# Weights prepared later and two at a time: the order of the weight split in a fused attention and MoE kernel

## The chip, the cores and the metric

One core of a Trainium2 chip runs the kernel. The metric is the device time of one execution in microseconds; the figure for a kernel is the median of its runs. Engine names below are those of the profile: PE is the matmul engine (PEld its weight loads), DVE the vector engine, ACT the scalar engine, POOL the GpSimd engine, SP the engine that issues most DMAs.

## What is computed

The reference runs a windowed attention with sink columns over 4 batches, 8 heads, 768 positions and a head size of 64, and sends the result through one gated two-layer block ("MoE" below, with a single expert):

```
scores = scale * q @ k^T, masked to (key < n_sink) or (0 <= query - key < window)
a = softmax(scores);  x = (a @ v), heads side by side: 3072 tokens x 512
out = ((x @ w_a) * (x @ w_b)) @ w_out          w_a, w_b: 512 x 1536, w_out: 1536 x 512
```

The three weights arrive in 64-bit floating point, so that each weight value is two 32-bit words, `lo` and `hi`. The rest is fp32.

## The kernel before, in words

The tokens are cut into eight chunks of 2 to 4 tiles of 128 rows (`CHUNKS`). `run` (L732 on) first computes the attention of chunk 0 alone (`first`, 4 tiles, 8 heads: 32 units of a head and a tile). Then `moe` (L674 on) works on one chunk after the other, and in the middle of the MoE of chunk c the generator `between` takes steps of the attention of chunk c+1. The matmuls of the MoE split each fp32 operand into a high and a low part of type fp32r and take three products (high by high, high by low, low by high).

The weights are cut into 12 blocks of each kind: `a` (w_a), `b` (w_b) and `o` (w_out), 128 x 512 values each, 36 in all. The MoE loop over j uses a_j (`half`, L685), then b_j, then o of j-1 (`project`, L694). For every block the kernel does the following, in four stages, each pinned in program order:

- `load_weight` (L289): one DMA of 512 KB into a raw tile;
- `weight_bits` (L297 to L299): two DVE operations on the high words and, between them, an ACT operation that scales the low words in place (L298);
- `weight_sum` (L307): a DVE integer addition that joins both;
- `weight_high` (L313): an ACT cast to fp32r, which writes the high part;
- `weight_low` (L318): a DVE subtraction, which writes the low part.

The high and low parts take the place of the raw tile in memory. `weights_to` moves this conveyor by steps: step k does bits of block k, sum of block k-1, high of block k-2 and low of block k-3. In the first attention a step is taken at every third generator step from `STEP0` = 18 on (18, 21, ..., 36: seven steps); in the first MoE one step is taken before every a, b and o. The order of the blocks is a0 b0 o0 a1 b1 o1 and so on.

In the attention of chunk 0 a unit's score matmul (L547) goes into PSUM; DVE takes the mask and the row minimum (L554); ACT takes the exponent (L556); DVE forms the sum's reciprocal (L558, L559) and multiplies (L561); PE transposes (L584); ACT copies (L585, tile ptx); PE multiplies with v (L601). The sink columns go through sct (L614), sk (L623) and an addition (L625). The head pairs' results xf are split into xh (ACT, L666) and xl (DVE, L667), which the first MoE matmuls read. PE, DVE and ACT each take their instructions strictly in order; a scheduler decides that order when the kernel is built, within the pins.

Of the kernel before, what the change touches and what calls it, by code (L numbers as in the profile page):

```python
# [7 lines left out]
F32 = mybir.dt.float32  # L8
BF16 = mybir.dt.bfloat16
F32R = mybir.dt.float32r  # L10
I32 = mybir.dt.int32
# [206 lines left out]
class Fast:  # L218
# [14 lines left out]
    def consts(self):  # L233
# [18 lines left out]
        self.wt, self.raw, self.wf, self.unchecked = {}, {}, {}, []  # L252

    def masks(self, val):

# [28 lines left out]
    def src(self, kind):  # L284
        return {"a": self.wa, "b": self.wb, "o": self.wo}[kind]

    def load_weight(self, kind, j):
        raw = self.wp.tile([P, 2 * DM], I32, tag=f"w_{kind}{j}", name=f"raw_{kind}{j}")
        self.nc.sync.dma_start(raw, self.src(kind)[j].bitcast(I32))  # L289
        self.raw[kind, j] = raw  # L290

    def weight_bits(self, kind, j):
        nc, pin = self.nc, self.tc.keep_in_program_order
        rv = self.raw[kind, j].rearrange("p (n c) -> p n c", c=2)
        lo, hi = rv[:, :, 0], rv[:, :, 1]
        f = self.io([P, DM], I32, f"wf_{kind}{j}")
# [4 lines left out]
        self.wf[kind, j] = f  # L301

    def weight_sum(self, kind, j):

        f = self.wf[kind, j]
        lo = self.raw.pop((kind, j)).rearrange("p (n c) -> p n c", c=2)[:, :, 0]
        self.tc.keep_in_program_order(self.nc.vector.tensor_tensor(f, f, lo, op=ALU.add))  # L307
        self.wf[kind, j] = f.bitcast(F32)

    def weight_high(self, kind, j):  # L310
        w = self.wp.tile([P, 2, DM], F32R, tag=f"w_{kind}{j}", name=f"w_{kind}{j}")
        self.wt[kind, j] = (w[:, 0, :], w[:, 1, :])
        self.tc.keep_in_program_order(self.nc.scalar.copy(w[:, 0, :], self.wf[kind, j]))  # L313

    def weight_low(self, kind, j):
        wh, wl = self.wt[kind, j]
        self.tc.keep_in_program_order(
            self.nc.vector.tensor_tensor(wl, self.wf.pop((kind, j)), wh.bitcast(F32), op=ALU.subtract))  # L318

    def check_weight(self, kind, j):  # L320

# [349 lines left out]
    def moe(self, row, nt, xf, between, weights_ahead, last, weights_split):  # L671
# [4 lines left out]
        outs = [self.ps.tile([P, DM], F32, tag=("o0", "o1", "o2", "av")[i], name=f"o{tag}_{i}") for i in range(nt)]  # L676

        def half(kind, j):
            wh, wl = self.wt[kind, j]
            ps = self.ps.tile([P, 4 * P], F32, tag=kind, name=f"{kind}{tag}_{j}")  # L680
            for kk in range(NK):
                ksl = slice(kk * P, (kk + 1) * P)
                xh, xl = xs[kk]
                for i, (w, x) in enumerate(((wh, xh), (wh, xl), (wl, xh))):
                    nc.tensor.matmul(ps[:, :n], lhsT=w[:, ksl], rhs=x[:, :n],  # L685
                                     start=kk == 0 and i == 0, stop=kk == NK - 1 and i == 2)
            return ps

        def project(j, gh, gl):
            wh, wl = self.wt["o", j]  # L690
# [40 lines left out]

    def run(self, scalars, verdict):  # L732
        chunks = CHUNKS
        order = [(k, j) for j in range(NJ) for k in "abo"]
        done, loaded = [0], [0]

        def weights_to(n, ahead):
            while loaded[0] < min(n + ahead, len(order)):
                self.load_weight(*order[loaded[0]])
                loaded[0] += 1  # L740
            while done[0] < min(n + D2, len(order) + D2):
                k = done[0]
# [7 lines left out]
        pairs = [self.wp.tile([P, 2, nt * P], F32, tag=f"w_{k}{NJ - 1}", name=f"xf0_{k}") for k in "bo"]  # L750
        xf = [x[:, i, :] for x in pairs for i in range(2)]
        first = self.attention(b, t0, nt, xf, exact=True, alone=True)
        next(first)
        val = scalars()
# [112 lines left out]
```

## Time and profile before

| | us |
|---|---|
| median of 3 runs | 802.18 |
| lowest and highest run | 800.78, 804.23 |
| the profiled execution, its own time | 800.92 |
| span of its trace, first to last instruction | 799.0 |

PE is busy for 785.5 us of the span, DVE for 433.3, ACT for 475.8 and POOL for 307.1. The chain of work that ended last lies on PE for 92% of the span, on DVE for 4% and on ACT for 3%. A matmul's busy time in such a trace has its pipeline in it: matmuls that follow each other start closer together than each one lasts, so that a gap of a few tenths of a microsecond between them does not show as idle time. What PE really takes for a group is read from the starts of the groups.

### The profile page before, as it was taken

How to read it: one execution, taken by the hardware profiler on the slowest of the kernel's cores; microseconds unless marked ns; L12 is line 12 of the kernel's file. 1: busy time of each engine (PE TensorE's matmuls, PEld its weight loads, DVE VectorE, ACT ScalarE, POOL GpSimd, SP SyncE). 2: the span in 40 equal slices, each digit the busy share in tenths (PEclk: the TensorE clock that was granted, in tenths of full speed). 3: DMA queues.
4: the chain of work that ended last, by engine and by line, in shares of the span. 5: the costliest groups of instructions: out<-in, count | busy, mean ns of one | idle time of the engine just before them, and what ended most of it. 6: DMA issues, size and time to landing. Idle time of an engine off the chain costs nothing.

```text
span 799.0 us, 13573 instructions
## 1 busy us (share of the span) xinstructions
PE 785.5 (98%) x4457; PEld 697.2 (87%) x4457; DVE 433.3 (54%) x1485; ACT 475.8 (60%) x1384; POOL 307.1 (38%) x425
## 2 busy tenths in 40 slices
PE   8989999999999999999999999999999999999997
PEld 5657777779899999999999999999999999999996
DVE  6889988835654565445653555535654457430101
ACT  5877676527764676467764777646764677641111
POOL 1111100416672644546642565606635366201120
PEclk9999999999999999999999999999999999999999
DMA  8868610122221242313333143322333132000001
GB/s 314 298 228 319 205 30 1 41 82 77 61 73 38 79 128 90 104 55 117 102 102 116 42 123 109 91 77 64 114 119 102 54 107 61 1 14 28 1 1 42
DMA packets 44779, 76.12 MB, mean 95 GB/s; under 512 B 4640, under 2 KB 24224, under 8 KB 44704
## 3 DMA queue, kind: packets, MB, share of 16 engines
q1 hardware_dynamic: 41648, 69.70, 27.2%
q10 hardware_dynamic: 3024, 5.51, 1.8%
q8 instruction: 36, 0.59, 0.3%
q14 instruction: 39, 0.32, 0.1%
q0 software_dynamic: 32, 0.00, 0.0%
HBM read 68.90 MB, written 6.29 MB: 94 GB/s over the span
## 4 chain that ended last, share of the span: by engine, by line
PE 92%; DVE 4%; ACT 3%; DMA 1%; issue 1%; POOL 0%; DVEq 0%; POOLq 0%; ACTq 0%
PE a L685 25%; PE o L694 24%; PE b L685 24%; PE t L450 4%; PE s L418 4%; PE av L466 3%; PE s L547 2%; PE av L601 2%; PE t L584 1%; PE t L601 1%; PE sk L491 1%; ACT p L425 1%; DVE g L710 0%; ACT xf L471 0%; DVE xf L472 0%
## 5 line engine op out<-in xcount | busy, mean ns | idle before, releaser
L685 PE MATMUL a<-xh,w_a 128*128 128x384 f32 (+2 forms) x768 | 218.2, 345 | 1.3 <-ACT xh L666 1.0
L685 PE MATMUL b<-xh,w_b 128*128 128x384 f32 (+2 forms) x768 | 215.8, 343 | 0.0
L694 PE MATMUL o<-w_o,gh 128*128 128x512 f32 x576 | 186.9, 404 | 0.0
L685 PEld LDWEIGHTS a<-xh,w_a 128*128 128x128 f32 x768 | 138.8, 188 | 8.2 <-issue 1.7
L715 POOL TENSOR_TENSOR gl<-g,gh 128x384 fp32r<-128x384 f32 (+1 forms) x70 | 68.2, 974 | 201.1 <-ACT gh L713 198.3
L685 PEld LDWEIGHTS b<-xh,w_b 128*128 128x128 f32 x768 | 138.8, 188 | 4.7 <-issue 1.2
L710 DVE TENSOR_TENSOR g<-b,g 128x384 f32<-128x384 f32 (+2 forms) x96 | 53.4, 557 | 146.2 <-PE b L685 133.3
L685 PE MATMUL b<-xl,w_b 128*128 128x384 f32 (+2 forms) x384 | 129.2, 336 | 0.0
L685 PE MATMUL a<-xl,w_a 128*128 128x384 f32 (+2 forms) x384 | 129.2, 336 | 0.0
L694 PEld LDWEIGHTS o<-w_o,gh 128*128 128x128 f32 x576 | 104.0, 188 | 19.3 <-issue 0.8
L694 PE MATMUL o<-w_o,gl 128*128 128x512 f32 x288 | 113.6, 395 | 0.0
L713 ACT CAST gh<-g 128x384 fp32r<-128x384 f32 (+2 forms) x96 | 49.3, 514 | 78.4 <-DVE g L710 76.5
L704 ACT COPY g<-a 128x384 f32<-128x384 f32 (+2 forms) x96 | 45.2, 471 | 72.9 <-PE a L685 70.3
L429 ACT ACTIVATE p<-p,st 128x128 f32<-128x128 f32 (+1 forms) x144 | 71.4, 496 | 26.4 <-DVE st L428 25.5
L425 ACT ACTIVATE p<-p,st 128x128 f32<-128x128 f32 (+1 forms) x144 | 71.6, 497 | 8.5 <-DVE st L423 8.4
L685 PEld LDWEIGHTS a<-xl,w_a 128*128 128x128 f32 x384 | 72.4, 189 | 2.3
L685 PEld LDWEIGHTS b<-xl,w_b 128*128 128x128 f32 x384 | 72.4, 188 | 1.6
L453 ACT CAST pt<-t 128x128 fp32r<-128x128 f32 (+1 forms) x144 | 50.4, 350 | 39.1 <-PE t L450 37.3
L454 DVE TENSOR_TENSOR pt<-t,pt 128x128 fp32r<-128x128 f32 (+1 forms) x144 | 57.2, 397 | 20.7 <-ACT pt L453 19.2
L694 PEld LDWEIGHTS o<-w_o,gl 128*128 128x128 f32 x288 | 54.1, 188 | 13.1 <-DVE gl L715 0.8
L568 POOL COPY sc<-p 128x8 f32<-128x8 f32 x32 | 15.7, 490 | 128.7 <-ACT p L563 86.6
L423 DVE CUSTOM_DVE_ANT_0 p<-s,mg 128x264 f32<-128x264 f32 x96 | 41.1, 429 | 34.2 <-PE s L418 34.0
(141 smaller groups left out, 1287.3 us busy)
## 6 DMA issues: line engine op xcount, KB each, us to landing
qr<-in_qT_dram SPq DMA_DIRECT2D x48, 192.0 KB, 2.6
raw_a<-in_wa_dram SPq DMA_DIRECT2D x12, 512.0 KB, 6.5
raw_b<-in_wb_dram SPq DMA_DIRECT2D x12, 512.0 KB, 6.6
raw_o<-in_wo_dram SPq DMA_DIRECT2D x12, 512.0 KB, 6.6
chk_a<-in_wa_dram SPq DMA_DIRECT2D x24, 256.0 KB, 2.7
chk_b<-in_wb_dram SPq DMA_DIRECT2D x24, 256.0 KB, 2.7
chk_o<-in_wo_dram SPq DMA_DIRECT2D x24, 256.0 KB, 2.8
out_dram<-os ACTq DMA_DIRECT2D x21, 256.0 KB, 2.1
```

The source lines that it names most:

```text
L418: nc.tensor.matmul(ps[:, :w], lhsT=q[:, i * P:(i + 1) * P], rhs=ks[:, c0:c0 + w], start=m == 0, stop=m == 1)
L423: nc.vector.tensor_tensor_reduce(out=p[:, :w], in0=ps[:, :w], in1=m, scale=-0.125, scalar=BIG, op0=ALU.add, op1=ALU.min, accum_out=st[:, 0:1])
L425: nc.scalar.activation(p[:, :w], p[:, :w], AF.Exp, bias=st[:, 0:1], scale=-1.0, accum_out=st[:, 1:2])
L429: nc.scalar.mul(p[:, :w], p[:, :w], st[:, 3:4])
L453: nc.scalar.copy(hs, tp[:, :n, :])
L454: nc.vector.tensor_tensor(ls, tp[:, :n, :], hs.bitcast(F32), op=ALU.subtract)
L685: nc.tensor.matmul(ps[:, :n], lhsT=w[:, ksl], rhs=x[:, :n], start=kk == 0 and i == 0, stop=kk == NK - 1 and i == 2)
L694: nc.tensor.matmul(outs[i], lhsT=g[:, sl], rhs=w, start=j == 0 and k == 0, stop=j == NJ - 1 and k == 2)
L704: nc.scalar.copy(g[:, :n], pa[:, :n])
L710: nc.vector.tensor_tensor(g[:, :n], pb[:, :n], g[:, :n], op=ALU.mult)
L713: nc.scalar.copy(gh[:, :n], g[:, :n])
L715: e.tensor_tensor(gl[:, :n], g[:, :n], gh[:, :n].bitcast(F32), op=ALU.subtract)
```

## The change

The order of the blocks becomes the order of their first use: a0 b0 a1 b1 o0 a2 b2 o1 and so on. In the first attention the steps begin at generator step 24 (24, 27, ..., 36: five steps). Blocks 0 and 1 and the last eight (28 to 35) go through the stages singly, as before. Blocks 2 to 27 go in 13 pairs: one raw tile holds two blocks, and each of the two bits operations, the ACT scaling, the sum, the cast and the subtraction works on 1024 words a partition instead of 512. For a pair, sum and high are issued in the same step, one after the bits, and low one step later. The pairs' intermediate value is one tile of its own in the weight pool (named wf), so the last four blocks, two of which use its place, are loaded only when the last pair is done. Before the product of a block in the MoE, low of the block three or four places later has been issued instead of four later.

```diff
-STEP0, STEPS = 18, 3
-AHEAD, LOADS = 3, 9
-D0, D1, D2 = 1, 2, 3
+STEP0, STEPS = 24, 3
+AHEAD, LOADS = 1, 11
+DELAY = 3
+SINGLE, PAIRS = 2, 14
...
+    def weight_bits(self, k, n):
         nc, pin = self.nc, self.tc.keep_in_program_order
...
+        lo, hi = self.words(k, n)
+        if n == 2:
+            if self.temp is None:
+
+                self.temp = self.wp.tile([P, 2 * DM], I32, tag=f"w{3 * NJ // 2 - 2}", name="wf")
+            f = self.temp
+        else:
+            f = self.io([P, DM], I32, f"wf{k}")
...
-        order = [(k, j) for j in range(NJ) for k in "abo"]
+
+        order = self.order = sorted(((k, j) for j in range(NJ) for k in "abo"), key=lambda w: 3 * w[1] + (0, 1, 5)["abo".index(w[0])])
...
+            wide = range(SINGLE, 2 * PAIRS)
             while loaded[0] < min(n + ahead, len(order)):
-                self.load_weight(*order[loaded[0]])
+                if loaded[0] >= len(order) - 4 and done[0] <= 2 * PAIRS:
+                    break
+                self.load_weight(loaded[0])
                 loaded[0] += 1
-            while done[0] < min(n + D2, len(order) + D2):
+            while done[0] < min(n + DELAY, len(order) + DELAY):
                 k = done[0]
-                for d, stage in ((D2, self.weight_low), (D1, self.weight_high), (D0, self.weight_sum), (0, self.weight_bits)):
-                    if 0 <= k - d < len(order):
-                        stage(*order[k - d])
                 done[0] += 1
+                singles = lambda d: 0 <= k - d < len(order) and k - d not in wide
+                if singles(3):
+                    self.weight_low(k - 3, 1)
+                if k % 2 == 0 and k - 2 in wide:
+                    self.weight_low(k - 2, 2)
+                if singles(2):
+                    self.weight_high(k - 2, 1)
+                if singles(1):
+                    self.weight_sum(k - 1, 1)
+                if k % 2 == 1 and k - 1 in wide:
+                    self.weight_sum(k - 1, 2)
+                    self.weight_high(k - 1, 2)
+                if singles(0):
+                    self.weight_bits(k, 1)
+                if k % 2 == 0 and k in wide:
+                    self.weight_bits(k, 2)
...
-                weights_to(done[0] + 1 - D2, 4 + D2)
+                weights_to(done[0] + 1 - DELAY, 4 + DELAY)
...
-                weights_to(max(s + AHEAD, done[0] + 1 - D2), LOADS)
+                weights_to(max(s + AHEAD, done[0] + 1 - DELAY), LOADS)
```

Line numbers from here on in the changed kernel are 17 higher in the attention and the MoE (L561 becomes L578, L666 becomes L683), and the weight stages move to L293 (load), L316 to L318 (bits), L325 (sum), L330 (high) and L335 (low).

The first place is the end of the first attention on DVE. A name such as p_0_7_2 is the softmax tile of chunk 0, head 7, tile 2; the last number of a name only counts tiles. Before, from the product of the last head's second tile to the first instruction behind that of its last tile:

```order
L561 TENSOR_SCALAR p_0_7_1_677<-p_0_7_1_677,st_0_7_1_678 128x264
L318 TENSOR_TENSOR w_b_624<-wf_b_518,w_b_624 128x512
L307 ISA wf_a_627<-raw_a_444,wf_a_627 128x1024
L297 TENSOR_SCALAR wf_b_694<-raw_b_446 128x512
L561 TENSOR_SCALAR p_0_7_2_700<-p_0_7_2_700,st_0_7_2_701 128x264
L299 SCALAR_TENSOR_TENSOR wf_b_694<-raw_b_446,wf_b_694 128x512
L558 TENSOR_SCALAR st_0_7_3_715<-st_0_7_3_715 128x1
L558 TENSOR_SCALAR st_4_0_0_879<-st_4_0_0_879 128x1
L559 RECIPROCAL st_0_7_3_715<-st_0_7_3_715 128x1
L559 RECIPROCAL st_4_0_0_879<-st_4_0_0_879 128x1
L561 TENSOR_SCALAR p_0_7_3_714<-p_0_7_3_714,st_0_7_3_715 128x264
L318 TENSOR_TENSOR w_o_691<-wf_o_576,w_o_691 128x512
```

With the change, the same stretch:

```order
L578 TENSOR_SCALAR p_0_7_1_654<-p_0_7_1_654,st_0_7_1_655 128x264
L325 ISA wf_604<-raw_549,wf_604 128x1024
L316 TENSOR_SCALAR wf<-raw_552 128x1024
L575 TENSOR_SCALAR st_0_7_2_677<-st_0_7_2_677 128x1
L575 TENSOR_SCALAR st_0_7_3_691<-st_0_7_3_691 128x1
L318 SCALAR_TENSOR_TENSOR wf<-raw_552,wf 128x1024
L576 RECIPROCAL st_0_7_2_677<-st_0_7_2_677 128x1
L576 RECIPROCAL st_0_7_3_691<-st_0_7_3_691 128x1
L684 TENSOR_TENSOR xl_2_765<-xf_117,xh_2_764 128x512
L578 TENSOR_SCALAR p_0_7_2_676<-p_0_7_2_676,st_0_7_2_677 128x264
L578 TENSOR_SCALAR p_0_7_3_690<-p_0_7_3_690,st_0_7_3_691 128x264
L335 TENSOR_TENSOR w_667<-wf_557,w_667 128x512
```

Ahead of the last product stood five bits, four sums and two subtractions of single blocks; now there are the bits of two single blocks and of one pair and two single sums. Low of the first block (w_667) has moved behind it.

The second place is the seam between attention and MoE on ACT, from the copy of the last head's result xf to the copy g_0 of the first a product. Before:

```order
L603 COPY xf_o<-av_0_7_756 64x512
L313 CAST w_b_773<-wf_b_694 128x512
L298 ACTIVATE raw_a_571<-raw_a_571 128x512
L585 COPY ptx_4_0_0_979<-t_4_0_0_980 128x256
L666 CAST xh_3_799<-xf_o 128x512
L313 CAST w_o_814<-wf_o_744 128x512
L298 ACTIVATE raw_b_621<-raw_b_621 128x512
L556 ACTIVATE p_4_0_1_924,st_4_0_1_925<-p_4_0_1_924,st_4_0_1_925 128x264
L704 COPY g_0_834<-a_0_821 128x512
```

With the change:

```order
L620 COPY xf_117<-av_0_7_728 64x512
L317 ACTIVATE raw_555<-raw_555 128x1024
L330 CAST w_718<-wf 128x1024
L573 ACTIVATE p_4_0_0_839,st_4_0_0_840<-p_4_0_0_839,st_4_0_0_840 128x264
L683 CAST xh_3_768<-xf_117 128x512
L721 COPY g_0_799<-a_0_786 128x512
```

The copy ptx_4_0_0 of the next chunk's first transposes no longer stands ahead of xh_3; an exponent and two operations on a pair do.

The third place is a piece of the first MoE on DVE, from the product g_2. Before:

```order
L710 TENSOR_TENSOR g_2_1029<-b_2_1054,g_2_1029 128x512
L299 SCALAR_TENSOR_TENSOR wf_a_990<-raw_a_809,wf_a_990 128x512
L318 TENSOR_TENSOR w_b_987<-wf_b_903,w_b_987 128x512
L307 ISA wf_a_990<-raw_a_809,wf_a_990 128x1024
L297 TENSOR_SCALAR wf_b_1012<-raw_b_811 128x512
L559 RECIPROCAL st_4_1_1_1034<-st_4_1_1_1034 128x1
L318 TENSOR_TENSOR w_o_1009<-wf_o_939,w_o_1009 128x512
L299 SCALAR_TENSOR_TENSOR wf_b_1012<-raw_b_811,wf_b_1012 128x512
L715 TENSOR_TENSOR gl_2_1069<-g_2_1029,gh_2_1068 128x512
```

With the change:

```order
L727 TENSOR_TENSOR g_2_964<-b_2_985,g_2_964 128x512
L335 TENSOR_TENSOR w_886<-wf,w_886 128x1024
L732 TENSOR_TENSOR gl_2_1000<-g_2_964,gh_2_999 128x512
L316 TENSOR_SCALAR wf<-raw_777 128x1024
L571 ISA p_4_2_0_1009,st_4_2_0_1010<-s_4_2_0_1007,mg 128x264
L571 ISA st_4_2_0_1010 128x1
L318 SCALAR_TENSOR_TENSOR wf<-raw_777,wf 128x1024
L575 TENSOR_SCALAR st_4_2_0_1010<-st_4_2_0_1010 128x1
L325 ISA wf<-raw_777,wf 128x2048
L576 RECIPROCAL st_4_2_0_1010<-st_4_2_0_1010 128x1
L335 TENSOR_TENSOR w_949<-wf,w_949 128x1024
```

Before, sum and low that stand next to each other belong to different blocks. Now low of a pair follows sum of the same pair, with the ACT cast between them and here one reciprocal on DVE.

## Rows read from the trace of the kernel before

**Rows 1.** Stretches: length; PE, PEld, DVE, ACT, POOL busy (count); granted clock; DMA.

```profile
28.30:50.80 22.50, 21.28 (x111) 12.68 (x110) 20.26 (x89) 18.80 (x55) 4.25 (x7) 1.00 0.82 295
50.80:61.30 10.50, 8.88 (x42) 5.67 (x41) 8.14 (x19) 6.11 (x14) 0.78 (x2) 1.00 0.50 163
61.30:165.00 103.70, 103.70 (x485) 80.28 (x486) 91.10 (x203) 65.08 (x144) 20.95 (x29) 1.00 0.35 119
165.00:179.10 14.10, 14.10 (x62) 11.40 (x63) 4.03 (x9) 4.80 (x10) 0.00 (x0) 1.00 0.14 43
```

**Rows 2.** Waits of PE, 61.3 to 179: total us, times, longest.

```profile
PE a L685 <- ACT g L704: 0.2, 1, 0.2
```

**Rows 3.** Chain that ended last, in the first MoE: start, us, what.

```profile
64.30 2.75 PE b L685 x12
67.05 2.80 PE o L694 x12
...
73.76 0.45 PE s L547 x2
```

**Rows 4.** Waits of DVE, 28.2 to 50.8: total us, times, longest.

```profile
DVE st L558 <- ACT p L556: 1.5, 3, 0.8
DVE p L554 <- PE s L547: 0.6, 1, 0.6
```

**Rows 5.** Timeline of DVE in the first attention: start, us, instruction.

```profile
48.04 0.69 DVE L318 TENSOR_TENSOR w_b<-wf_b,w_b 128x512 fp32r<-128x512 f32 x1
48.64 0.68 DVE L307 CUSTOM_DVE_ANT_0 wf_a<-raw_a,wf_a 128x1024 uint16<-128x1024 uint16 x1
49.24 0.42 DVE L297 TENSOR_SCALAR wf_b<-raw_b 128x512 int32<-128x512 int32 x1
49.58 0.35 DVE L561 TENSOR_SCALAR p<-p,st 128x264 f32<-128x264 f32 x1
49.84 0.68 DVE L299 SCALAR_TENSOR_TENSOR wf_b<-raw_b,wf_b 128x512 int32<-128x512 int32 x1
50.44 0.21 DVE L558 TENSOR_SCALAR st<-st 128x1 f32<-128x1 f32 x2
...
50.82 0.36 DVE L561 TENSOR_SCALAR p<-p,st 128x264 f32<-128x264 f32 x1
```

**Rows 6.** Instruction groups by shape: busy us, mean ns, idle before.

```profile
L710 DVE TENSOR_TENSOR g<-b,g 128x512 f32<-128x512 f32 x12 | 8.3, 688 | 4.5 <-PE b L685 4.0 <-ACT w_o L313 0.3
L710 DVE TENSOR_TENSOR g<-b,g 128x256 f32<-128x256 f32 x12 | 5.1, 423 | 10.8 <-PE s L418 6.9 <-PE b L685 2.9 <-PE sk L491 1.0
L713 ACT CAST gh<-g 128x512 fp32r<-128x512 f32 x12 | 7.4, 618 | 6.5 <-DVE g L710 6.5
L713 ACT CAST gh<-g 128x256 fp32r<-128x256 f32 x12 | 4.9, 407 | 5.0 <-DVE g L710 3.2 <-DMA out_dram<-os 1.6
```

**Rows 7.** Timeline of ACT at the seam.

```profile
58.80 0.62 ACT L313 CAST w_o<-wf_o 128x512 fp32r<-128x512 f32 x1
59.32 0.68 ACT L298 ACTIVATE raw_b<-raw_b 128x512 int32<-128x512 uint32 x1
```

**Rows 8.** Timeline of PE at the seam; in brackets the idle time and its releaser.

```profile
53.92 0.65 PE L601 MATMUL av<-ptx,vx 128*64 128x128 f32 x4 [0.35 <-ACT ptx L585]
...
56.10 0.69 PE L623 MATMUL sk<-sct,vsx 16*128 16x256 f32 x2
...
57.54 0.38 PE L584 MATMUL t<-ident,p 128*128 128x128 f32 x2
58.95 0.50 PE L685 MATMUL a<-xh,w_a 128*128 128x512 f32 x1 [1.03 <-ACT xh L666]
...
61.26 0.51 PE L685 MATMUL a<-xh,w_a 128*128 128x512 f32 x1 [0.22 <-ACT g L704]
```

**Rows 9.** Timeline of SP: the last of fourteen weight loads issued before the seam.

```profile
34.17 0.48 SPq L289 DMA_DIRECT2D raw_b<-in_wb_dram  x1
```

**Rows 10.** Timeline of DVE late in the first MoE, beside POOL work.

```profile
150.49 1.42 DVE L318 TENSOR_TENSOR w_o<-wf_o,w_o 128x512 fp32r<-128x512 f32 x1
```

More of the change, by code (lines that the diff above doesn't have):

```diff
@@ L251, in consts @@
         self.pt, self.kr = None, {}
-        self.wt, self.raw, self.wf, self.unchecked = {}, {}, {}, []
+        self.wt, self.raw, self.wf, self.temp, self.unchecked = {}, {}, {}, None, []
     def masks(self, val):
@@ L285, in src, with load_weight, words, parts @@
         return {"a": self.wa, "b": self.wb, "o": self.wo}[kind]
[L287 to L292, printed above, removed]
-        nc, pin = self.nc, self.tc.keep_in_program_order
-        rv = self.raw[kind, j].rearrange("p (n c) -> p n c", c=2)
-        lo, hi = rv[:, :, 0], rv[:, :, 1]
-        f = self.io([P, DM], I32, f"wf_{kind}{j}")
+    def load_weight(self, k):
+        if k % 2 == 0:
+            self.raw[k // 2] = self.wp.tile([P, 2, 2 * DM], I32, tag=f"w{k // 2}", name=f"raw{k // 2}")
+        kind, j = self.order[k]
+        self.nc.sync.dma_start(self.raw[k // 2][:, k % 2], self.src(kind)[j].bitcast(I32))
+    def words(self, k, n):
+        rv = self.raw[k // 2][:, k % 2:k % 2 + n].rearrange("p i (n c) -> p (i n) c", c=2)
+        return rv[:, :, 0], rv[:, :, 1]
+    def parts(self, k, n):
+        w = self.wt[k // 2][:, :, k % 2:k % 2 + n].rearrange("p c i n -> p c (i n)")
+        return w[:, 0], w[:, 1]
+    def weight(self, kind, j):
+        return self.parts(self.order.index((kind, j)), 1)
+    def weight_bits(self, k, n):
+        nc, pin = self.nc, self.tc.keep_in_program_order
+        lo, hi = self.words(k, n)
[5 more added lines that the diff above has]
+            f = self.io([P, DM], I32, f"wf{k}")
         pin(nc.vector.tensor_scalar(f, hi, 3, 0x3FFFFFF8, op0=ALU.logical_shift_left, op1=ALU.bitwise_and))
@@ L300, in weight_bits, with weight_sum, weight_high, weight_low @@
                                            op0=ALU.bitwise_and, op1=ALU.bitwise_or))
[L301 to L316, printed above, removed]
+        self.wf[k] = f
+    def weight_sum(self, k, n):
+        f = self.wf[k]
+        self.tc.keep_in_program_order(self.nc.vector.tensor_tensor(f, f, self.words(k, n)[0], op=ALU.add))
+    def weight_high(self, k, n):
+        if k % 2 == 0:
+            self.wt[k // 2] = self.wp.tile([P, 2, 2, DM], F32R, tag=f"w{k // 2}", name=f"w{k // 2}")
+        self.tc.keep_in_program_order(self.nc.scalar.copy(self.parts(k, n)[0], self.wf[k].bitcast(F32)))
+    def weight_low(self, k, n):
+        wh, wl = self.parts(k, n)
         self.tc.keep_in_program_order(
-            self.nc.vector.tensor_tensor(wl, self.wf.pop((kind, j)), wh.bitcast(F32), op=ALU.subtract))
+            self.nc.vector.tensor_tensor(wl, self.wf.pop(k).bitcast(F32), wh.bitcast(F32), op=ALU.subtract))
     def check_weight(self, kind, j):
@@ L678, in half @@
         def half(kind, j):
-            wh, wl = self.wt[kind, j]
+            wh, wl = self.weight(kind, j)
             ps = self.ps.tile([P, 4 * P], F32, tag=kind, name=f"{kind}{tag}_{j}")
@@ L689, in project @@
         def project(j, gh, gl):
-            wh, wl = self.wt["o", j]
+            wh, wl = self.weight("o", j)
             for i in range(nt):
@@ L733, in run @@
         chunks = CHUNKS
-        order = [(k, j) for j in range(NJ) for k in "abo"]
+        order = self.order = sorted(((k, j) for j in range(NJ) for k in "abo"), key=lambda w: 3 * w[1] + (0, 1, 5)["abo".index(w[0])])
         done, loaded = [0], [0]
         def weights_to(n, ahead):
+            wide = range(SINGLE, 2 * PAIRS)
             while loaded[0] < min(n + ahead, len(order)):
-                self.load_weight(*order[loaded[0]])
+                if loaded[0] >= len(order) - 4 and done[0] <= 2 * PAIRS:
+                    break
+                self.load_weight(loaded[0])
                 loaded[0] += 1
-            while done[0] < min(n + D2, len(order) + D2):
+            while done[0] < min(n + DELAY, len(order) + DELAY):
                 k = done[0]
-                for d, stage in ((D2, self.weight_low), (D1, self.weight_high), (D0, self.weight_sum), (0, self.weight_bits)):
-                    if 0 <= k - d < len(order):
-                        stage(*order[k - d])
                 done[0] += 1
+                singles = lambda d: 0 <= k - d < len(order) and k - d not in wide
[14 more added lines that the diff above has]
+                    self.weight_bits(k, 2)
         b, t0, nt = chunks[0]
-        pairs = [self.wp.tile([P, 2, nt * P], F32, tag=f"w_{k}{NJ - 1}", name=f"xf0_{k}") for k in "bo"]
-        xf = [x[:, i, :] for x in pairs for i in range(2)]
+        x = self.wp.tile([P, NK, nt * P], F32, tag=f"w{3 * NJ // 2 - 1}", name="xf0")
+        xf = [x[:, i, :] for i in range(NK)]
         first = self.attention(b, t0, nt, xf, exact=True, alone=True)
```

## The prediction

> **What bounds the kernel now.** I first read the busy time by stretches [rows 1], then the waits of each engine inside a stretch, and last the timelines at the places where the change puts something else. In the first MoE (61.3 to 165 us) PE is busy for all of 103.70 us at a granted clock of 1.00, and from 61.3 to 179 its only listed wait is one of 0.2 us [rows 2]. Since busy time can hide small gaps, I also look at starts: twelve matmuls take 2.75 or 2.80 us [rows 3], 0.23 us each, chunk after chunk of the loop. This stage is bound by PE; weight work on DVE and ACT lies beside it, with DVE at 91.1 of 103.7 us.
>
> The end of the first attention is another case. From 28.3 to 50.8 us DVE is busy for 20.26 of 22.50 us [rows 1], and of the rest 1.5 us are waits for ACT's exponent and 0.6 for PE [rows 4]. Here the weight work stands in the same queue as the softmax. The reader is to see in rows 5 how: a product of the softmax (L561) stands between operations on weights, each of which delays it by its whole slot. The stage's end, 50.8 to 61.3, has PE waits of 0.35, 1.03 and 0.22 us [rows 8]. So the change can gain before 61 us and can lose after it.
>
> **The change part by part.** All times are for the profiled execution (800.92 us, span 799.0); it lies 1.26 us under the median of 802.18, and I carry the difference over to the median.
>
> Slots on DVE, from start to start [rows 5]: subtraction 0.60 (48.04 to 48.64), sum 0.60, first bits operation 0.34, second bits operation 0.60 (49.84 to 50.44, where the next instruction of the queue starts). A single block thus costs 2.14 us, of which bits are 0.94.
>
> 1. *Weight work taken from in front of the last softmax product* (50.82 us, [rows 5]). Before, five bits, four sums and two subtractions have been done by then: 5 x 0.94 + 4 x 0.60 + 2 x 0.60 = 8.3 us. Now it is two single bits (1.88), two single sums (1.20) and the bits of one pair. A pair's operation is not in the trace. The nearest rows are one operation of two inputs at 512 and at 256 columns [rows 6]: 688 and 423 ns, so 512 columns more cost 0.53 us, and a slot grows from 0.60 to 1.13. The bounds are 0.60 (the second half free) and 1.20 (nothing saved); I take 1.13, and for the first bits operation the upper bound, 0.68. The pair's bits are 1.81, the sum 4.89, and DVE loses 3.4 us of weight work on the path. Since DVE is 90% busy there, I count all of it.
>
> 2. *ACT's part of the same.* The 1.5 us in which DVE waits for the exponent [rows 4] come partly from casts and scalings in ACT's queue (a cast's slot is 0.52 us, a scaling is busy for 0.68, [rows 7]). Fewer of them remain ahead of the last exponent. Bounds 0 and 1.5; I take 0.8.
>
> 3. *The seam.* From the last product at 50.82 to the end of a_0 and b_0 at about 61.04 (61.26 less the idle 0.22, [rows 8]) are 10.2 us. In them PE also does 1.1 us for the next chunk (two score matmuls of 0.45 [rows 3] and a pair of transposes, some 0.2), which now come later; that leaves 9.1. Now PE has behind that product: transposes 0.2, the ptx copy 0.35, two groups of av matmuls (0.65 each, [rows 8]), sink work 0.9 (0.69 in [rows 8], and two transposes), and 22 of the 24 matmuls of a_0 and b_0 at 0.23, 5.1: together 7.8. The wait of 1.03 us for xh goes: before, xh stood on ACT behind the next chunk's ptx, whose transposes PE took at 57.54 [rows 8]; now pair work stands there. What is late next is the cast of w_718, 0.94 (0.52 plus 0.42 by the cast's rows in [rows 6]), but eight matmuls (1.85 us) now stand between the sink matmul and the first use of xh_3. Gain 1.3; bounds 0 and 1.6 (all three waits).
>
> 4. *The first MoE.* It has to take what was pushed out. DVE's weight work over all blocks is 36 x 2.14 = 77.0 before, and 13 pairs at 4.07 plus ten singles, 74.3, after. Done by the end of the seam: before 14.1 (the 8.3 and three subtractions, three sums, two bits and a first bits operation), after 8.4. Left over for the MoE are 62.9 and 65.9: 3.0 us more, against 12.6 us in which DVE is free [rows 1]. That is hidden by PE, at no cost. New is that a pair's subtraction stands close behind its sum and must wait for the cast between them, up to 1.04 us (0.62 plus 0.42) where nothing fills it. The weights are still ready three blocks ahead, 3 x 3.3 us of PE (117.8 us for 36 blocks, [rows 1]), so I count 0.4 us, less than the cast of one pair; bounds 0 and 2, two pairs unfilled. Weight loads cost nothing: both orders have issued fourteen by the seam, at 34.2 us in this trace [rows 9]; in the MoE the transfer engines are busy for 0.35 of the time [rows 1].
>
> The VectorE: DVE Perf Modes page of the Trainium skill (The TRN2 errata section) gives an fp32 operation of two inputs (N + 151) / 0.96 ns. That agrees with the 688 ns at 512 columns. Read as a cost per instruction it would make a pair save 0.16 us per operation; the slots of rows 5, 0.60 us start to start, show that most of this is already overlapped, so 0.07. By the page, term 4 would be 0 and the forecast 796.7.
>
> Sum: 3.4 + 0.8 + 1.3 - 0.4 = 5.1 us. From 800.92 that gives 795.8 for an execution like the profiled one, and **797.1 us** for the median.
>
> **The rivals.** *The gain is mostly taken back at the seam.* Between the products of tiles 1 and 2 of the last head DVE now has a single sum, a pair's bits and xl_2, 0.60 + 1.81 + 0.60 = 3.0 us. Before, PE filled such waits with matmuls of a_0; now low of the first block stands behind the products, and PE's order has two of them there, 0.5 us. If PE waits for the rest, 2.5 us of the 5.1 go: 799.6. For it speaks the order on DVE; against it, that DVE was already the late one in rows 4 and 5.
>
> *POOL meets the last weights.* Late in the MoE a subtraction took 1.42 us [rows 10] instead of 0.69 while POOL prepared the next chunk. If such preparation starts earlier, up to 24 operations of two inputs on the last eight blocks are stretched by half of that 0.73 us, 9 us of DVE, most of it inside the 10 us that DVE is idle after 165 [rows 1]; even if 4 us reached PE, the time would be 801. The SBUF — State Buffer page of the Trainium skill (Who interferes with whom) says that a DVE instruction with two SBUF inputs and a GpSimd one that reads SBUF lock each other out; the 1.42 agrees with it.
>
> *Slower: DVE and ACT take turns on the pairs.* Sum waits for the scaling, low for the cast, and nothing fills either. With w us lost per pair, the MoE grows by 3.0 + 13w - 12.6, against the 5.5 of terms 1 to 3: slower than before from w = 1.2 on. A whole cast alone (1.04) stays under it, 800.6; with half of a scaling (0.68 + 0.42) on top, w is 1.6, the MoE grows by 11.2, and the time is 807.9. Against it speaks that products, gl and row minima stand between many sums and their subtractions, and that ACT has 65 of 104 us of work.
>
> That the weights would not move at all is excluded by the order shown above.
>
> **How the numbers follow.** A change of 0.5% (4.0 us, under 798.2 or over 806.2) is about what a measurement of this kernel can tell from none. Forecast 0.60; gain taken back at the seam 0.30; POOL 0.03; slower by turns 0.07. Only part of the last passes 806.2, and part of the forecast's own spread lies above 798.2: faster 0.56, same 0.39, slower 0.05. The sum with the gaining bounds is 3.4 + 1.5 + 1.6 = 6.5 us, 795.7; with the others 3.4 - 2 = 1.4, 800.8. Half the spread of three runs allows another microsecond below: 794.8 to 801.0, which leaves out most of the slower case and little else.
>
> **What would show it.** Right: the last softmax product some 4 us earlier (near 46.6), a_0 and b_0 done near 54.5 with less of the next chunk in front, no wait for xh of a microsecond, and PE without gaps up to the second MoE, whose first matmul comes at about 174 instead of 179.1. Pair slots of 1.13 us show term 1's price. Wrong: PE waits at the transposes of tile 2 of head 7 (second case); PE waits in the MoE for w, gl or b's product g, with DVE waiting for casts (slower); stretched DVE operations after 140 us (POOL). The forecast fails if DVE was not the bound of the attention's end: then the last product comes less than 2 us earlier.

## The result, and the profile after

| | before | changed |
|---|---|---|
| median, us | 800.80 (5 runs) | 796.09 (5 runs) |
| lowest and highest, us | 800.78, 804.23 | 795.74, 797.02 |
| profiled execution, own time and span, us | 800.92, 799.0 | 797.02, 795.1 |

The changed kernel takes 0.993 of the time (95% interval 0.991 to 0.995): 4.7 us less between the medians, against 5.1 forecast. It is faster by 0.5 to 0.9%.

The profiled execution of the changed kernel is the slowest of its five, 0.9 us over their median, and the loss lies ahead of the first operation on a weight. Two places are good marks for taking this apart: the pair of sink transposes skt at 27 us, ahead of the first weight operation of either kernel, and the first matmul of the second MoE, the first with 256 columns. PE's timeline of the kernel before has them at:

```profile
27.16 0.39 PE L612 MATMUL skt<-ident,sc 128*16 128x128 f32 x2
...
178.96 0.28 PE L685 MATMUL a<-xh,w_a 128*128 128x256 f32 x1
```

and that of the changed kernel at:

```profile
28.11 0.39 PE L629 MATMUL skt<-ident,sc 128*16 128x128 f32 x2
...
175.34 0.28 PE L702 MATMUL a<-xh,w 128*128 128x256 f32 x1
```

The first mark is 0.95 us later (the last section shows what happened there), the second 3.62 earlier. From mark to mark it is 151.80 us before and 147.23 after: the change is worth 4.57 us inside this stretch. All times of stages below are counted from the first mark.

What [rows 5] showed of DVE before the last softmax product now reads, in DVE's timeline (start, us, instruction):

```profile
44.16 0.69 DVE L325 CUSTOM_DVE_ANT_0 wf<-raw,wf 128x1024 uint16<-128x1024 uint16 x1
44.76 0.69 DVE L316 TENSOR_SCALAR wf<-raw 128x1024 int32<-128x1024 int32 x1
...
45.49 1.22 DVE L318 SCALAR_TENSOR_TENSOR wf<-raw,wf 128x1024 int32<-128x1024 int32 x1
46.63 0.22 DVE L576 RECIPROCAL st<-st 128x1 f32<-128x1 f32 x2
46.76 0.67 DVE L684 TENSOR_TENSOR xl<-xf,xh 128x512 fp32r<-128x512 f32 x1
47.35 0.62 DVE L578 TENSOR_SCALAR p<-p,st 128x264 f32<-128x264 f32 x2
47.89 0.68 DVE L335 TENSOR_TENSOR w<-wf,w 128x512 fp32r<-128x512 f32 x1
48.49 1.22 DVE L325 CUSTOM_DVE_ANT_0 wf<-raw,wf 128x2048 uint16<-128x2048 uint16 x1
```

The products of the last two tiles stand back to back; the second starts 0.27 us behind the first, at 47.62. From the mark that is 19.51 us, against 23.66 before: 4.15 earlier. The pair's second bits operation is busy for 1.22 us and takes a slot of 1.14, from 45.49 to 46.63.

The waits of PE from 28 to 180 us (total us, times, longest) are these three, and the one of 1.03 us for xh [rows 8] is gone:

```profile
PE a L702 <- ACT w L330: 0.8, 1, 0.8
PE t L601 <- DVE st L576: 0.7, 1, 0.7
PE av L618 <- ACT ptx L602: 0.2, 1, 0.2
```

By stretches, with the columns of [rows 1], cut at the products of the last two tiles, at the end of a_0 and b_0, and just behind the first matmul of the second MoE:

```profile
28.30:47.35 19.05, 17.48 (x107) 12.27 (x106) 17.20 (x80) 15.29 (x48) 2.06 (x6) 1.00 0.86 304
47.35:56.72 9.37, 9.01 (x44) 6.41 (x45) 7.17 (x15) 5.24 (x11) 2.11 (x2) 1.00 0.44 163
56.72:175.51 118.79, 118.79 (x553) 92.57 (x552) 96.54 (x176) 72.48 (x140) 21.04 (x30) 1.00 0.35 120
```

The reader is to see that PE is busy for all of the first MoE, as before, though DVE waits there for the new neighbour of a pair's subtraction. Its list of waits from 60 to 165 begins

```profile
DVE w L335 <- ACT w L330: 5.5, 9, 1.4
```

nine waits for the cast, 0.6 us each on average, and PE has no wait listed in that time.

### The profile page after: what moved, and what is told of

Same layout as the page of the kernel before. It is cut to its first block, busy times and chain, and to the rows that moved or that the text cites. A ratio compares the mean times of both kernels' runs of the same rounds, so it can differ in the third digit from the quotient of the medians.

```text
span 795.1 us, 13521 instructions
## 1 busy us (share of the span) xinstructions
PE 782.0 (98%) x4457; PEld 698.1 (88%) x4457; DVE 430.4 (54%) x1433; ACT 473.5 (60%) x1358; POOL 306.4 (39%) x425
## 4 chain that ended last, share of the span: by engine, by line
PE 92%; DVE 3%; ACT 2%; DMA 1%; issue 1%; POOL 1%; DVEq 0%; POOLq 0%; ACTq 0%
PE o L711 24%; PE b L702 24%; PE a L702 24%; PE t L467 4%; PE s L435 4%; PE av L483 3%; PE s L564 3%; PE av L618 1%; PE t L601 1%; PE t L618 1%; PE sk L508 1%; ACT p L442 1%; DMA nw_raw<-in_nw_dram 0%; DVE g L727 0%; ACT xf L488 0%
## 5 line engine op out<-in xcount | busy, mean ns | idle before, releaser
L702 PE MATMUL a<-xh,w 128*128 128x384 f32 (+2 forms) x768 | 217.3, 344 | 0.8 <-ACT w L330 0.8
L702 PE MATMUL b<-xh,w 128*128 128x384 f32 (+2 forms) x768 | 215.2, 343 | 0.0
L711 PE MATMUL o<-w,gh 128*128 128x512 f32 x576 | 186.4, 404 | 0.0
L702 PEld LDWEIGHTS a<-xh,w 128*128 128x128 f32 x768 | 138.7, 188 | 7.3 <-issue 1.2
L702 PEld LDWEIGHTS b<-xh,w 128*128 128x128 f32 x768 | 138.8, 188 | 4.3 <-issue 0.7
L702 PE MATMUL a<-xl,w 128*128 128x384 f32 (+2 forms) x384 | 129.1, 336 | 0.0
L702 PE MATMUL b<-xl,w 128*128 128x384 f32 (+2 forms) x384 | 129.0, 336 | 0.0
L711 PEld LDWEIGHTS o<-w,gh 128*128 128x128 f32 x576 | 103.9, 188 | 19.2 <-issue 0.8
L711 PE MATMUL o<-w,gl 128*128 128x512 f32 x288 | 113.7, 395 | 0.0
L702 PEld LDWEIGHTS a<-xl,w 128*128 128x128 f32 x384 | 72.4, 189 | 2.4
```

Of the source, the lines that this page charges most:

```text
L702: nc.tensor.matmul(ps[:, :n], lhsT=w[:, ksl], rhs=x[:, :n], start=kk == 0 and i == 0, stop=kk == NK - 1 and i == 2)
L711: nc.tensor.matmul(outs[i], lhsT=g[:, sl], rhs=w, start=j == 0 and k == 0, stop=j == NJ - 1 and k == 2)
```

## The experiments

Theory D: DVE's queue sets the end of the first attention, and the gain is the weight work that the later point takes out of it. Its rivals: P, the pairs bring the gain; S, the seam and the order of blocks do. Later ones stand with the runs. The table has for each run the DVE weight work W in front of the last product (from the order of the queue and the prediction's slots), the start of that product and of the second MoE, both from the first mark in the profiled execution, and the median with its ratio to before.

| run | W | product | second MoE | median | ratio, 95% interval |
|---|---|---|---|---|---|
| before | 8.30 | 23.66 | 151.80 | 800.8 to 801.7 | |
| changed | 4.89 | 19.51 | 147.23 | 796.09 | 0.991 to 0.995 |
| e1_step18 | 10.16 | 25.53 | 152.30 | 802.14 | 0.9999 to 1.0018 |
| e2_singles | 4.02 | 18.71 | 147.35 | 795.98 | 0.9916 to 0.9947 |
| e3_before_step24 | 4.02 | 18.70 | 147.37 | 796.13 | 0.9916 to 0.9947 |
| e4_before_order | 8.30 | 23.67 | 151.75 | 801.93 | 0.9987 to 1.0020 |
| e5_step21 | 6.62 | 21.72 | 150.07 | 798.38 | 0.9948 to 0.9976 |
| e6_step27 | 2.48 | 18.36 | 149.67 | 799.80 | 0.9967 to 0.9990 |
| e7_singles26 | 2.48 | 18.54 | 147.54 | 796.59 | 0.9927 to 0.9954 |
| e8_scalar_load | 4.89 | 19.51 | 147.52 | 796.24 | 0.9923 to 0.9951 |
| e9_more_dve | 6.25 | 20.85 | 148.49 | 798.22 | 0.9948 to 0.9975 |
| e10_more_act | 4.89 | 19.51 | 147.26 | 797.32 | 0.9923 to 0.9959 |
| e11_singles23 | 4.02 | 19.45 | 149.57 | 798.13 | 0.9931 to 0.9968 |
| e12_step24_load | 4.02 | 18.71 | 147.55 | 796.41 | 0.9916 to 0.9954 |

### The parts one by one: e1 to e4

e1, the changed kernel from the old point:

```diff
-STEP0, STEPS = 24, 3
+STEP0, STEPS = 18, 3
```

> The changed kernel with the old starting point (STEP0 18); its order of blocks and its pairs stay. Theory L (the gain is the later point: weight work leaves the queue in front of the last softmax product): by DVE's order 8.35 us of weight work stand in front of that product (two single bits 1.88, two single sums 1.20, a pair's bits 1.81, a pair's sum 1.13, two single subtractions 1.20, a pair's 1.13) against 8.3 in the kernel before, so term 1 is gone; the time is within 1 us of before, 799.5 to 801.5, and the last product comes at 50 to 51 us. Rival P (the gain is the pairs, fewer and cheaper operations): 796 to 798. Rival S (the gain is the seam and the order of blocks, with xh no longer behind the next chunk's work): 797 to 799.

The gain is gone, 802.14 us, so P and S fall as the cause of it. The median is above the expected 801.5; the kernel before had 801.6 beside this run. The product came later than the expected 50 to 51 us, at 53.78, because theory D's number counted to the product of tile 2; to the last one it is 10.16 us: the bits of a second pair, 1.81 us, stand between. With that the product fits, 1.87 us later than before for 1.86 us more work. The second MoE is only 0.50 us later than before, so that 1.4 us came back behind the product; what gave them back was not separated.

e2, the changed kernel without pairs (no block is in the range of pairs any more):

```diff
-SINGLE, PAIRS = 2, 14
+SINGLE, PAIRS = 28, 14
```

> The changed kernel with every block handled singly; later point and order of blocks stay. Theory L: in front of the last product stand four bits and two sums, 4 x 0.94 + 2 x 0.60 = 4.96 us against 4.89, so the gain stays; the first MoE gets 36 x 2.14 - 5 = 72 us of DVE work at most, less than 7 us more than before, against 12.6 idle, hidden: 796 to 797.5. Rival P: most of the gain is lost, 799 to 801. A third way: without pairs DVE or ACT becomes late in the first MoE and PE waits there for weights; then the last product is as early as in the changed kernel and the time is 798 or more.

795.98 us: the pairs bring nothing that can be measured. Over 61.3 to 165 us the first row below is this run, with the columns of [rows 1]

```profile
61.30:165.00 103.70, 103.70 (x487) 80.14 (x486) 90.64 (x206) 66.86 (x148) 17.88 (x27) 1.00 0.34 116
```

and the next is the changed kernel:

```profile
61.30:165.00 103.70, 103.70 (x487) 80.40 (x486) 89.22 (x163) 64.20 (x125) 17.64 (x26) 1.00 0.33 119
```

Pairs save 1.4 us of DVE and 2.7 of ACT, all of it beside a PE that is busy for 103.70 of 103.70 us. In front of the last product DVE's queue has three bits and two sums, W = 4.02, and not the four bits of the expectation (the same holds for e3). The product is 0.80 us earlier than in the changed kernel, but the second MoE is not (147.35 and 147.23): below the changed kernel's 4.89 us, less work bought nothing here.

e3, the kernel before with the later point alone:

```diff
-STEP0, STEPS = 18, 3
+STEP0, STEPS = 24, 3
```

> The kernel before with only the later point (STEP0 24). Its order of blocks (a, b, o by turns), single operations and the catching up at the head of the first MoE (AHEAD 3) stay. Theory L: 4.96 us of weight work in front of the last product instead of 8.3, so 3.3 us and some of ACT's part come back: 796.5 to 798, last product at 47 to 48. Rival S: the later point alone leaves the seam as late as before, or moves work into it: 799.5 to 802, with PE waits at the seam of 2 us or more in all. If the order of blocks or the pairs are needed to keep the first MoE fed, the first attention ends early but PE waits for weights after 60 us.

796.13 us: one number of the old kernel gives the whole gain. PE has no wait of more than 0.7 us from 28 to 180 us; the wait for xh is gone here too, though neither the pairs nor the new order of blocks are in this kernel. In its ACT timeline, too, no ptx copy stands ahead of xh_3 any more; the scheduler's order at the seam changed with the point alone.

e4, the kernel before with the new order of blocks alone:

```diff
-        order = [(k, j) for j in range(NJ) for k in "abo"]
+        order = sorted(((k, j) for j in range(NJ) for k in "abo"), key=lambda w: 3 * w[1] + (0, 1, 5)["abo".index(w[0])])
```

> The kernel before with only the new order of blocks (a, b of a slice two slices ahead of its o). Theory L and rival P: same queue lengths in front of the last product, so within 0.5 us of before, 800.3 to 801.5. Rival S: 797 to 799.5, if it is the order that lets the seam run.

No difference beside the 801.6 us of the kernel before (ratio 1.0003), and the profiled execution is that of before to within 0.05 us at both places.

### The point itself: e5, e6, e7 and e11

All four change the STEP0 of 24 in the changed kernel: e5 to 21 and e6 to 27; e7 to 26 and e11 to 23, both with the edit of e2.

```diff
-STEP0, STEPS = 24, 3
+STEP0, STEPS = 21, 3
```

> The changed kernel with an earlier point, STEP0 21. By DVE's order the weight work in front of the last softmax product (tile 3 of head 7) is now 2 single bits, 2 single sums, 1 single subtraction, a pair's bits and a pair's sum: 1.88 + 1.20 + 0.60 + 1.81 + 1.13 = 6.62 us. The runs so far give, for that work and the start of that product (start-up shift of about 1 us taken off): 4.02 and 45.9 (singles, point 24), 4.89 and 46.7 (changed kernel), 8.3 and 50.8 (before), 10.16 and 52.8 (changed kernel, point 18; the expectation of that run counted up to tile 2 only): 1.1 us later per us of work. Theory D (DVE's queue sets the end of the first attention, each us of weight work costs 1.1 there): product near 48.7, time 797.5 to 798.5. Rival P (what counts is whether the casts of the first blocks are late on ACT, not DVE's work): casts come earlier here, so 795 to 796.

798.38, as theory D had it. The product is 2.21 us later for 1.73 us more work. The second MoE is even 2.84 later in the profiled execution. PE's clock fell in it from 42 to 48 us, partly ahead of the product, which takes part of both numbers; the last section shows the rows.

> The changed kernel with a still later point, STEP0 27: 2 single bits and 1 sum, 2.48 us of weight work in front of the last product. Theory D alone: product at about 44.2, and the time falls by another 2 to 2.7 us, 793.4 to 794.2. Theory B (in the changed kernel PE has become the bound from 46 us on, since it has both last tiles' transposes and products with V and the whole of a_0 and b_0 behind it): the product comes earlier but PE's end of b_0 moves by no more than the 0.8 us of the wait for the first cast, time 795.2 to 796.3. Rival W (too late: weights of the first slices are late, PE waits at a_1, b_1 or the first o): 797 or more, with PE waits for w after 50 us.

> Every block singly and STEP0 26: also 2.48 us of weight work in front of the last product, but smaller slots behind it. Theory D alone: 794.0 to 794.5 against 796.0 of singles at point 24 (1.54 us less work, 1.1 each). Theory B: 795.2 to 796.3. Rival W: 797 or more.

Neither gains. With 2.4 us less work than the changed kernel the product of e6 comes only 1.15 us earlier, and with 1.54 less than e2 that of e7 only 0.17: from about 4 us down, DVE's weight work no longer sets it one for one. What PE waits for in e7, from 28 to 180 us, is ACT:

```profile
PE av L618 <- ACT xf L620: 0.7, 1, 0.7
PE av L618 <- ACT ptx L602: 0.7, 2, 0.5
PE sk L640 <- ACT xf L620: 0.2, 1, 0.2
```

So theory B was right for later points in that nothing more is gained: 796.59, 0.6 us over e2. In e6, with pairs, the time, 799.80, is in the range of rival W but its sign is missing: none of PE's waits from 28 to 180 us is for w. The two longest, 0.9 us each, are for ACT's copy xf and for its cast gh. A cast and a scaling of a pair have come ahead of that copy. ACT's timeline at the seam

```profile
47.74 0.62 ACT L330 CAST w<-wf 128x512 fp32r<-128x512 f32 x1
48.26 1.16 ACT L317 ACTIVATE raw<-raw 128x1024 int32<-128x1024 uint32 x1
49.45 0.58 ACT L620 COPY xf<-av 64x512 f32<-64x512 f32 x1
```

and PE's, where the sink product waits for that copy:

```profile
50.08 0.69 PE L640 MATMUL sk<-sct,vsx 16*128 16x256 f32 x2 [0.87 <-ACT xf L620]
```

> Every block singly, STEP0 23. The weight work on DVE in front of the last product is the same as with point 24 (three bits and two sums, 4.02 us), but on ACT the first block's cast now stands ahead of the exponents of the last two tiles and of the copy of head 6's result, where PE waited for it by 0.8 us in the changed kernel and in the run of singles at point 24. If that wait is on the path: 795.1 to 795.6. If the exponents behind the cast give it back: 795.8 to 796.4. If the casts ahead of them delay the last product by a whole cast and a scaling (1.2): 797.

The opposite attempt, an earlier cast for the first matmul of a_0, also loses: the wait of 0.8 us goes, but the product comes 0.74 us later than in e2 with the same W, and PE waits 0.91 us for a ptx copy in its place. From the first mark to the last product DVE waits 0.8 us for exponents, and not at all in e2, which fits the casts ahead of them; but the edit also put a second xl (0.60 us) between the products of tiles 1 and 2, so the casts are not shown to be the cause. The three lowest of seven executions, 796.84 to 796.91, are 0.9 us over e2, at a granted clock of 0.999; the rest of the median's 2.1 us comes with executions at 0.997 or less (last section). Point 24 is the best of those tried.

### DVE alone and ACT alone: e9 and e10

e9 repeats one operation:

```diff
-        pin(nc.vector.tensor_scalar(f, hi, 3, 0x3FFFFFF8, op0=ALU.logical_shift_left, op1=ALU.bitwise_and))
+        for _ in range(5 if k == 1 else 1):
+            pin(nc.vector.tensor_scalar(f, hi, 3, 0x3FFFFFF8, op0=ALU.logical_shift_left, op1=ALU.bitwise_and))
```

> The changed kernel, with the first bits operation of the second block (L316, 512 columns, slot 0.34 us) issued five times over instead of once: 4 x 0.34 = 1.36 us more on DVE in front of the last softmax product, nothing more on ACT. Theory D (DVE's queue alone delays the product, 1 us per us, and the end of the first attention follows it): product 1.3 to 1.5 us later than in the changed kernel, time 797.0 to 797.7. Theory B (in the changed kernel PE is already the bound there, which is why points later than 24 brought nothing): product later, time within 0.4 us of 796.1. Rival A (of the gain, most came from ACT's casts and scalings that left the front): also near 796.1, and the next kernel, with more on ACT, is the slower.

The product moves by 1.34 us for 1.36 us of work, the second MoE by 1.26, and the median by 2.1, more than theory D gave. The rest comes behind the second MoE's start: counted from the first mark, the last instruction that computes is 1.78 us later than in the changed kernel. Why stays open. The run contradicts theory B at point 24 for added work: DVE delays the end of the first attention one for one, while less work (e2, e6, e7) brings nothing. The changed kernel lies at the corner between the two.

e10 adds two scalings on ACT:

```diff
         pin(nc.scalar.activation(lo, lo.bitcast(U32), AF.Copy, scale=2.0 ** -29))
+        if k == 1:
+            for _ in range(2):
+                pin(nc.scalar.activation(self.io([P, DM], I32, "more"), hi.bitcast(U32), AF.Copy, scale=2.0 ** -29))
```

> The changed kernel with two more scalings of 512 columns on ACT (into a buffer that nothing reads) behind the scaling of the second block: about 2 x 0.6 = 1.2 us more on ACT in front of the exponents of the last two tiles, nothing more on DVE. Term 2 of the prediction counted 0.8 us for three casts and three scalings (some 3.6 us of ACT) that left the front, so 0.2 us per us: 796.2 to 796.6. Rival A: the exponents and the first cast wait for all of it, 797 or more. Theory B or slack on ACT: 796.1.

The median says rival A, the trace says slack: product and second MoE stand at 19.51 and 147.26 us from the mark, as in the changed kernel (19.51 and 147.23), and PE's three waits are the same. The difference lies before the mark, at 28.29 us in this execution, as it does in the profiled one of the changed kernel. Of the six executions the two with a granted clock of 0.998 or more took 796.05 and 796.44, the four with 0.996 or 0.997 took 797.25 to 797.56. So 1.2 us of scalings at that place cost nothing. But ACT had room there: in the changed kernel it waits for PE's transposes, 0.24 and 1.20 us, between 41.35 and 43.16 us, and the two scalings run in that gap. The run does not show what scalings cost where ACT is busy.

### The start: e8 and e12

In e8 (the changed kernel) and e12 (the kernel before, with point 24 too) the load of the two scalars goes to another queue:

```diff
-        nc.gpsimd.dma_start(raw, nw)
+        nc.scalar.dma_start(raw, nw)
```

> The changed kernel with the small load of the two scalars issued by ACT's queue instead of POOL's; all else stays. In the profiled execution of the changed kernel that load was read on DVE at 5.00 us (4.49 in the kernel before), PE had no work from 5.24 to 7.12, its granted clock was 0.85 and then 0.50 between 6 and 10 us, and the tenth softmax group was 0.96 us later than before. Theory N (the start hangs on this load): DVE reads it about 0.5 us earlier, since it need not wait for POOL's queue at 1.35 us, the first scores are taken up that much earlier, PE's gap before 8 us shrinks, and the time falls by 0.3 to 1.0 us, 795.1 to 795.8. Rival: the mask's chain on DVE or the key and query loads set the start, 796 to 796.4, no change.

> The kernel before with two edits: the later point (STEP0 24, 796.1 us alone) and the scalars' load on ACT's queue. With that load the tenth group of products with V in the first attention came at 25.25 us instead of 25.9 (profiled execution of the run with the load in the changed kernel). If that 0.65 us reaches the end: 795.2 to 795.6. If the end does not follow, as the median of that run (796.24) suggests: 796.0 to 796.4.

DVE reads the scalars at 3.50 us in e8, and the first mark comes at 26.49 us, against 27.16 in the kernel before, whose start had no fall of the clock; but the time is that without the edit, 796.24, and 796.41 in e12. In e12 the next wait is already to be seen in PE's timeline, for the load of a query block:

```profile
8.61 0.46 PE L547 MATMUL s<-kx,qx 128*128 128x128 f32 x2 [1.36 <-DMA qx<-in_qT_dram]
```

Its first mark is at 27.34. Where e8 lost its 0.65 us again can be read from the profiled executions: 0.29 up to the second MoE (147.52 against 147.23 from the mark), and 0.7 behind the last instruction that computes, from its end to the end of the span: 789.00 to 794.4, or 5.4 us, against 4.7 in the changed kernel (790.38 to 795.1). In e12 it is 5.5. Whether the load's queue causes this stays open. No version was found that beats the changed kernel; e2 and e3 equal it.

## Why the prediction was right, and where it was off

The forecast, 797.1 in a range of 794.8 to 801.0, was right in sign and in its main mechanism, weight work that leaves DVE's queue in front of the last softmax product; the size, 5.1 us, was measured at 4.7. That 797.1 lies 1.0 us above the measured 796.09 comes from the level: the forecast carried over the 1.26 us by which the median of three runs lay above the profiled execution, and with five runs the median of the kernel before is 800.80, below that execution. For an execution like the profiled one it had said 795.8. By its steps:

1. *Weight work in front of the last product, 3.4 us: right.* e9 shows the price, 1.34 us of delay per 1.36 us of DVE work, and e1 1.87 per 1.86. The 1.13 us that was taken for the slot of a pair's operation, between the bounds 0.60 and 1.20, is what the trace shows (1.14). The Trainium skill (VectorE: DVE Perf Modes, The TRN2 errata section) gives an fp32 operation of two inputs (1024 + 151) / 0.96 ns, an estimate of 1.22 us, and the busy time agrees (1.22); the slot is shorter by what overlaps. That pairing saves only some 0.07 us per operation stands by the slots, 2 x 0.60 against 1.14; e2, which has no pairs and the same time, shows that this saving does not count in the time.

2. *ACT's part, 0.8 us: the size fits, the cause is in part argued.* The product came 4.15 us earlier, terms 1 and 2 said 4.2, so 0.75 are left for it. From the first mark to the last product, DVE's waits in the changed kernel are

```profile
DVE sct L631 <- PE skt L629: 1.9, 2, 1.0
DVE p L571 <- PE s L564: 0.5, 2, 0.4
```

The 1.5 us of waits for the exponent [rows 4] are gone, and the waits for PE's skt have grown from 1.0 to 1.9. Two of the three exponent waits before, 0.40 and 0.36 us (to 35.14 and 44.52 on DVE), come behind a cast in ACT's timeline:

```profile
33.98 0.62 ACT L313 CAST w_a<-wf_a 128x512 fp32r<-128x512 f32 x1
34.51 0.52 ACT L556 ACTIVATE p<-p,st 128x264 f32<-128x264 f32 x1
...
42.93 0.62 ACT L313 CAST w_o<-wf_o 128x512 fp32r<-128x512 f32 x1
43.45 0.66 ACT L298 ACTIVATE raw_b<-raw_b 128x512 int32<-128x512 uint32 x1
44.01 0.39 ACT L556 ACTIVATE p<-p,st 128x128 f32<-128x128 f32 x1
```

The longest, 0.77 us, has no weight work directly ahead of it on ACT, but a copy that waited for PE. So casts and scalings can account for 0.76 of the 1.5 us, close to the term. Ahead of the last exponent stood three casts and four scalings before, and stand no cast and two scalings now. Which of the two kinds counted was not measured: e10's added scalings fell into a gap of ACT, and e11 moved more than a cast.

3. and 4. *The seam, 1.3, and the first MoE, -0.4: together 0.9, measured 0.4.* From the last product to the second MoE it is 128.14 us before and 127.72 after. Counted as term 3 counts it, the seam gave nothing: 9.1 us before, without the next chunk's 1.1, and 9.1 after, from 47.62 to 56.72. The 0.4 then lies behind it, where term 4 had expected a loss of 0.4 and PE has no wait. Since the 1.1 is an estimate, this split is good to a few tenths. So the seam was mis-sized: the wait for xh went as predicted, but the 7.8 us of PE work behind the product were counted as if all of tile 2 had been done. PE's timeline of the changed kernel around the product at 47.62:

```profile
46.09 0.50 PE L702 MATMUL a<-xh,w 128*128 128x512 f32 x1 [0.82 <-ACT w L330]
46.43 0.39 PE L702 MATMUL a<-xl,w 128*128 128x512 f32 x1
46.66 0.60 PE L564 MATMUL s<-kx,qx 128*128 128x264 f32 x2
47.29 0.92 PE L618 MATMUL av<-ptx,vx 128*64 128x128 f32 x6
48.14 0.66 PE L601 MATMUL t<-ident,p 128*128 128x128 f32 x4
49.04 0.65 PE L618 MATMUL av<-ptx,vx 128*64 128x128 f32 x4 [0.24 <-ACT ptx L602]
...
56.49 0.40 PE L702 MATMUL b<-xh,w 128*128 128x512 f32 x1
56.72 0.61 PE L564 MATMUL s<-kx,qx 128*128 128x264 f32 x2
```

Part of a group of six matmuls with V (to 48.14) and the transposes of both last tiles were still to come, 9.1 us from 47.62 to 56.72 instead of 7.8. The two products arrive together, and only two matmuls of a_0 stood in front of them, behind a wait of 0.82 us for the first cast. The second case of the prediction had the gain taken back by a wait at the transposes of tile 2. That wait did not come: the products were done at 47.97, and the transposes at 48.14 have no wait listed. What took the seam's 1.3 us back is work left over behind the product.

Of what was to show it, the last product near 46.6 came at 47.62, which is 46.67 without the start's 0.95, and pair slots of 1.13 at 1.14; a_0 and b_0 were done at 55.8 (without the 0.95) rather than 54.5, and the second MoE began 4.6 us earlier rather than 5. The case of turns between DVE and ACT shows in the list of waits, but small: 5.5 us over the twelve pairs' subtractions between 60 and 165 us, 0.5 each, less than half of its threshold of 1.2. POOL's case has its sign but no cost: from 140 to 180 us four DVE operations are stretched, to between 0.88 and 1.53 us, against six in the kernel before, and PE has no wait listed from 60 to 180 us.

## What to carry to other kernels

Before making side work cheaper, ask at which point of the queue it stands: here the same operations, moved behind the last softmax product, gave the whole gain (e3), and cheaper ones in the old place gave none (e1). Moving such work paid here only up to the corner where another engine's own work takes over, and a few steps to either side of the point in use show where that is. When a change is worth half a per cent, compare stages from a mark ahead of it, because the median can also carry what happened elsewhere in the execution.

## What was not expected of the hardware

PE's clock can fall behind a short idle time, and that decides part of the times above. In the changed kernel's profiled execution the scalars were read at 5.00 us instead of 4.49, and PE had a gap of 1.88 us before 7.12. The granted clock (third from the end of each row) was 1.00 in the kernel before and here

```profile
6.00:8.00 2.00, 0.88 (x2) 0.30 (x2) 1.87 (x10) 0.49 (x2) 0.00 (x0) 0.85 0.96 312
8.00:10.00 2.00, 2.00 (x7) 1.40 (x6) 1.68 (x13) 1.22 (x4) 0.00 (x0) 0.50 1.04 379
10.00:12.00 2.00, 2.00 (x10) 1.61 (x10) 1.87 (x13) 1.87 (x8) 0.19 (x1) 0.80 1.05 404
```

0.50 is the lower of its two levels, 1.2 of 2.4 GHz. e10 (a gap of 1.56 us) and e1 (1.37) show the same fall from 8 us on. It also happens at the seam. In e5, behind a wait of 1.26 us,

```profile
40.93 0.33 PE L601 MATMUL t<-ident,p 128*128 128x128 f32 x1 [1.26 <-DVE sct L631]
```

the clock was

```profile
42.00:44.00 2.00, 1.87 (x10) 1.39 (x10) 1.31 (x9) 1.47 (x6) 0.19 (x1) 0.84 1.04 345
44.00:46.00 2.00, 2.00 (x6) 1.20 (x6) 2.00 (x12) 1.66 (x6) 0.00 (x0) 0.50 1.10 376
46.00:48.00 2.00, 2.00 (x11) 1.33 (x11) 2.00 (x4) 0.85 (x4) 0.00 (x0) 0.81 0.88 284
```

and in e11, behind the wait of 0.91 us,

```profile
48.00:50.00 2.00, 2.00 (x9) 1.16 (x7) 0.86 (x3) 0.01 (x1) 0.00 (x0) 0.50 1.00 388
50.00:52.00 2.00, 2.00 (x9) 1.54 (x9) 2.00 (x5) 0.65 (x2) 0.00 (x0) 0.66 0.44 167
```

The length of the wait does not decide it alone: the clock stayed at 1.00 behind the wait of 1.03 us for xh in the kernel before, of 1.01 us in e1 (at 43.26) and of 1.36 us in e12 (at 8.61). What else decides is not shown here.

The executions of one kernel spread with the clock: beside e1 to e4 the kernel before took 800.5 to 801.6 us where the recorded clock was 0.998 or more (but for one of 802.3 and one of 802.0), and 803.5 to 804.6 where it was 0.992 to 0.994. The runs e2, e3 and e7, in whose profiled executions no single PE wait at the seam is over 0.9 us and no clock fell there, stay within 0.9 us each. But e8, e9 and e12, without a fall in the profiled execution too, spread by 1.3, 1.9 and 1.0 us, so one calm profile does not tell the spread. That the wait for xh in the kernel before brings its falls is a guess: no profiled execution of it has one.

A POOL copy of 128x8 elements took 0.19 us at 42.70 and far longer at 47.77, in POOL's timeline of the changed kernel:

```profile
42.70 0.19 POOL L585 COPY sc<-p 128x8 f32<-128x8 f32 x1 [1.42 <-DVE st L576]
47.77 2.11 POOL L585 COPY sc<-p 128x8 f32<-128x8 f32 x2 [4.88 <-DVE p L578]
```

The two at 47.77 took 2.11 us, while DVE had the single subtraction from 47.89 and the pair's sum up to 49.71. The Trainium skill (SBUF — State Buffer, Who interferes with whom) says that a DVE instruction with two SBUF inputs and a GpSimd one that reads SBUF lock each other out, and the trace agrees. It cost PE nothing here; the longest wait for such a copy in any run was 0.4 us (e9).
